# Seven half-width products for a pair of hidden blocks, in the last four batches of a linear attention with a cos-gated MLP

## The chip, the core and the metric

The kernel runs on one core of a Trainium2 chip. Its time is the device time of one execution in microseconds. The engines are TensorE (PE in the rows, its weight loads PEld), VectorE (DVE), ScalarE (ACT), GpSimd (POOL) and SyncE (SP), whose queue issues most of the DMAs; ScalarE's queue issues a few.

## What is computed

The reference, cut to its core (8 batches, 8 heads, 576 rows, head size 64; d_model 512, d_ff 2048):

```python
q_s = exp(q - max(q, -1)); q_s /= sum(q_s, -1) + 1e-9        # over d
k_s = exp(k - max(k, 2));  k_s /= sum(k_s, 2) + 1e-9         # over s
kv = einsum('bhsd,bhse->bhde', k_s, v)
attn = einsum('bhsd,bhde->bhse', q_s, kv)
x = attn.transpose(0, 2, 1, 3).reshape(4608, 512)
h = x @ w_in
out = (h * cos(h)) @ w_out
```

q, k and v are fp32; the two weights come in as 8-byte words, which the kernel turns into fp32 values itself. "The first product" below is x @ w_in, "the second" (g = h cos h) @ w_out.

## The kernel before

**Tiling.** 512 of the 576 rows of each batch are worked as one block; the 64 that are left of each of the eight batches go to DRAM (`x_left`) and come back as a ninth block, batch 8. The hidden dimension is cut into 16 blocks f of 128. A unit is one batch and one f; `order` (L922 to L926) lists all 144. Batches 0 and 1 go through f 0 to 7 and then f 8 to 15 in turn, while the weights arrive; batches 2 to 8 go through all 16. A batch b from 2 on so has units 16 b to 16 b + 15.

**Precision.** Each operand of a product is kept as two halves, high and low, in float32r, and a product is three matmuls: high by high, high by low, low by high. In the first product of a unit (`unit1`, `g1`, L928 to L950) four blocks of 128 rows of w_in are summed, so 12 matmuls of 512 columns go into one PSUM tile `h`. ScalarE then counts turns (L954), VectorE takes the rest (L958), ScalarE the cosine (L964), VectorE multiplies by h (`gate`, L970), ScalarE rounds the high half (L979) and VectorE subtracts for the low half (L985). The second product (`unit2`, L1012 to L1051) has 12 matmuls, three for each of four PSUM tiles `acc`, which are kept through a whole batch and copied out at its end (`out_rows`, L1053). Units with u below F2 = 6 make the second product in one fp32 matmul for each tile (L1021).

**Attention of a batch.** `attend` (L1114) makes k's exponentials (`k_exps`), kv (`kv_rows`, `k_steps`), q's softmax (`q_steps`), the transpose of q by way of DRAM for batches from 2 on (`q_out`, `q_in`, `q_blocks`) and x = q kv (`x_steps`, L739 to L897), four head pairs p for each batch. `x_hi` and `x_lo` (L813, L826) split x into its two halves straight from PSUM. The attention of batch b is woven into the units of batch b - 1. For batch 0 it stands alone, as nothing else can run; its 14 loads follow the list `seq` on SP's queue, or on ScalarE's for those in `actq`.

**PSUM.** There are eight tiles of 2 KB a partition: four `acc`, two `att` (attention) and two `h`. One unit's h is drained while the next unit fills the other one.

**SBUF.** Weights w_in and w_out of every f stay in SBUF, in both halves, from their conversion (`convert`, L378) to the end.

**Order.** Every step is entered in a `Plan` (L56) with its engine, an estimated length, what it reads and writes, and for some a due time (`when(pos)`, T0 + unit x pos, L1111). `order` (L157) lists the steps by a schedule that these lengths give, and the kernel is written out in that order by hand; so each engine's queue, and that of SP, has a fixed sequence. At the end (L1217 to L1221) two units of second product stand after the last first product, and the last two units follow tile by tile.

## Time and profile before

| what | us |
|---|---|
| median of three runs (842.96 to 844.15) | 843.15 |
| the profiled execution | 844.75 |
| its span, from the first instruction to the last | 842.9 |
| TensorE busy in the span | 815.1 |
| VectorE busy | 569.9 |
| ScalarE busy | 504.0 |
| GpSimd busy | 42.5 |

The page gives busy times of each engine, 40 slices of the span, the DMA queues, the chain of work that ended last, and the costliest groups of instructions. A matmul's recorded time is longer than the distance to the next one, since matmuls are pipelined; so TensorE's pace is read from starts. A timeline row merges instructions of one line that follow each other: its second number is the time from the first start to the last end. The mean granted clock of TensorE is 0.998.

### The profile page before, as it was taken

The numbers are of one execution on the slowest core, as the hardware profiler recorded it, in microseconds if no ns is written. First come the engines' busy times: TensorE is split into PE (matmuls) and PEld (weight loads), VectorE is DVE, ScalarE is ACT, GpSimd is POOL, SyncE is SP. The second block draws the span as 40 slices with busy tenths as digits, with TensorE's granted clock in tenths as the row PEclk, the third lists the DMA queues.
The fourth block names the chain that finished last, engine by engine and source line by source line (L and its number), as shares of the span: only waits on it lengthen the run. The fifth ranks groups of instructions, "written<-read, shape, count | busy, mean of one in ns | idle before, by whom it ended". The sixth has DMA issues, their size and how long they took to land.

```text
span 842.9 us, 11862 instructions
## 1 busy us (share of the span) xinstructions
PE 815.1 (97%) x4308; PEld 701.5 (83%) x4308; DVE 569.9 (68%) x920; ACT 504.0 (60%) x823; POOL 42.5 (5%) x161
## 2 busy tenths in 40 slices
PE   1899999999999999999999999999999999999997
PEld 1665788888888888888888888888888888888886
DVE  6979999998598558755876587547763454333443
ACT  3889999866456747564766456745743363334331
POOL 1300200001000000010001000000000000000000
PEclk9999999999999999999999999999999999999999
DMA  8891592246264034502450236023410030001001
GB/s 241 261 270 31 161 327 79 75 114 158 74 165 109 17 81 123 119 17 66 115 142 13 64 73 169 23 49 85 134 32 1 4 101 0 1 1 51 1 0 51
DMA packets 167227, 75.76 MB, mean 90 GB/s; under 512 B 111360, under 2 KB 157952, under 8 KB 167168
## 3 DMA queue, kind: packets, MB, share of 16 engines
q1 hardware_dynamic: 163600, 72.48, 31.8%
q10 hardware_dynamic: 3568, 2.52, 1.0%
q8 instruction: 34, 0.56, 0.3%
q14 instruction: 25, 0.20, 0.1%
HBM read 55.31 MB, written 19.66 MB: 89 GB/s over the span
## 4 chain that ended last, share of the span: by engine, by line
PE 88%; ACT 5%; DMA 3%; DVE 1%; issue 1%; SPq 1%; ACTq 0%; DVEq 0%
PE h L948 41%; PE acc L1028 40%; PE x_False L804 3%; PE kv L622 2%; PE acc L1021 2%; DMA q<-in_q_dram 2%; ACT raw_io L392 1%; DMA raw_i<-in_moe_w_in_dram 1%; DMA v_sb<-in_v_dram 1%; ACT kt L964 0%; ACT ghi L979 0%; ACT kt L954 0%; ACT raw_io L397 0%; ACT o L1077 0%; ACT q L712 0%
## 5 line engine op out<-in xcount | busy, mean ns | idle before, releaser
L948 PE MATMUL h<-x,w_i 128*128 128x512 f32 x1056 | 242.7, 381 | 0.8 <-DVE g L970 0.8
L948 PEld LDWEIGHTS h<-x,w_i 128*128 128x128 f32 x1056 | 198.8, 189 | 30.3 <-DVE g L970 1.2
L1028 PE MATMUL acc<-w_o,ghi 128*128 128x512 f32 x744 | 221.7, 380 | 0.3 <-ACT o L1077 0.3
L958 DVE SCALAR_TENSOR_TENSOR kt<-kt,h 128x512 f32<-128x512 int32 x144 | 99.0, 687 | 104.8 <-ACT kt L954 104.3
L954 ACT ACTIVATE kt<-h 128x512 int32<-128x512 f32 x144 | 86.2, 599 | 132.5 <-PE h L948 128.3
L1028 PEld LDWEIGHTS acc<-w_o,ghi 128*128 128x128 f32 x744 | 139.9, 189 | 20.3 <-ACT o L1077 0.7
L1028 PE MATMUL acc<-w_o,glo 128*128 128x512 f32 x372 | 141.1, 379 | 0.0
L970 DVE TENSOR_TENSOR kt<-kt,h 128x512 f32<-128x512 f32 x138 | 94.7, 686 | 57.7 <-ACT kt L964 56.8
L979 ACT CAST ghi<-kt 128x512 fp32r<-128x512 f32 x136 | 84.3, 620 | 76.3 <-DVE kt L970 38.7
L985 DVE TENSOR_TENSOR glo<-kt,ghi 128x512 fp32r<-128x512 f32 x136 | 93.9, 691 | 51.2 <-ACT ghi L979 50.7
L964 ACT ACTIVATE kt<-kt 128x512 f32<-128x512 f32 x144 | 91.5, 635 | 56.8 <-DVE kt L958 56.4
L948 PE MATMUL h<-x,w_io 128*128 128x512 f32 x480 | 109.6, 379 | 0.0
L1028 PE MATMUL acc<-w_io,ghi 128*128 128x512 f32 x344 | 102.8, 381 | 0.0
L948 PEld LDWEIGHTS h<-x,w_io 128*128 128x128 f32 x480 | 90.1, 189 | 12.4
L1028 PEld LDWEIGHTS acc<-w_o,glo 128*128 128x128 f32 x372 | 70.3, 189 | 10.4 <-DVE glo L985 0.4
L1028 PEld LDWEIGHTS acc<-w_io,ghi 128*128 128x128 f32 x344 | 63.8, 189 | 8.7
L1028 PE MATMUL acc<-w_io,glo 128*128 128x512 f32 x172 | 65.2, 379 | 0.0
L1028 PEld LDWEIGHTS acc<-w_io,glo 128*128 128x128 f32 x172 | 32.5, 189 | 4.6
L804 PE MATMUL x_False<-qt,kvw 128*128 128x288 f32 x176 | 35.5, 323 | 0.5 <-ACT kvw L659 0.5
L964 ACT ACT_TABLE_LOAD x26 | 33.4, 1283 | 0.5
L804 PEld LDWEIGHTS x_False<-qt,kvw 128*128 128x128 f32 x176 | 28.7, 195 | 5.8 <-issue 2.1
L560 POOL PARTITION_ALL_REDUCE m<-m x32 | 26.6, 874 | 118.4 <-DVE m L554 107.7
(114 smaller groups left out, 783.0 us busy)
## 6 DMA issues: line engine op xcount, KB each, us to landing
out_dram<-o SPq DMA_DIRECT2D x32, 256.0 KB, 2.1
q<-in_q_dram SPq DMA_DIRECT2D x31, 256.0 KB, 3.4
k<-in_k_dram SPq DMA_DIRECT2D x14, 512.0 KB, 4.2
qb<-q_rows SPq DMA_DIRECT2D x96, 72.0 KB, 2.4
q_rows<-q SPq DMA_DIRECT2D x24, 256.0 KB, 2.3
raw_i<-in_moe_w_in_dram SPq DMA_DIRECT2D x11, 512.0 KB, 5.3
v<-in_v_dram SPq DMA_DIRECT2D x22, 256.0 KB, 3.5
raw_o<-in_moe_w_out_dram SPq DMA_DIRECT2D x10, 512.0 KB, 5.8
```

The lines of the kernel that those rows point to most:

```text
L560: nc.gpsimd.partition_all_reduce(T["m", b, p0][:, hs].rearrange("p h d -> p (h d)"), T["m1", b, p0][:, hs].rearrange("p h d -> p (h d)"), ...
L622: nc.tensor.matmul(x[h * D : (h + 1) * D, odd : odd + vt.shape[1]], t[:, h, c, :], vt, start=(c == CM), stop=(c == CM - 1),)
L804: nc.tensor.matmul(t[:, 0:HALF], a, c[:, cs] if whole else woven(c[:, cs]), start=(n == 0), stop=(n == len(parts) - 1 and not again))
L948: nc.tensor.matmul(o, a, woven(x), start=(c == 0 and n == 0), stop=(c == KC - 1 and n == 2))
L954: nc.scalar.activation(t, T["h", u], AF.Identity, bias=0.25, scale=1.0 / TWO_PI)
L958: nc.vector.scalar_tensor_tensor(t.bitcast(F32), t, -TWO_PI, T["h", u], op0=ALU.mult, op1=ALU.add)
L964: nc.scalar.activation(t, t, AF.Sin, bias=0.5 * math.pi)
L970: nc.vector.tensor_mul(o, t, T["h", u])
L979: nc.scalar.copy(t, T["kt", u].bitcast(F32))
L985: nc.vector.tensor_sub(t, T["kt", u].bitcast(F32), T["gh", u].bitcast(F32))
L1021: nc.tensor.matmul(T["acc", j], T["g", u][:, js], T["wc", "o", f][:, 0], start=first, stop=last)
L1028: nc.tensor.matmul(T["acc", j], a[:, js], woven(w), start=(first and n == 0), stop=(last and n == 2))
```

## The change

Up to batch 4 the products stay as they are. From batch 5 on (`SB=5`) the units come in pairs, f and f + 1, whose first product is a product of a 512 x 256 block of w_in with the 512 columns of x. Both are cut in two each way, which gives four blocks of w_in and four of x, and the four blocks of the result are made with seven products of blocks instead of eight (Strassen's method, in the form with shared sums). A block of x is 256 rows of d_model by 256 of the 512 columns; a product of blocks is 6 matmuls of 256 columns (two blocks of 128 rows, three matmuls each).

- The weight sums are made once, in eight groups (`combine`), one every six units from unit 32 on, and written with the plain blocks to DRAM (`combined`, 56 operands of 128 x 2 x 256 fp32). From batch 5 on each pair reads its seven operands back into the places where w_in's f 6 to 13 stood; f 0 to 5 give room for the sides of x, f 14 and 15 for g of half of the units.
- The sums of x's blocks (`x_parts`): x goes from PSUM to SBUF as fp32 (`x_f32`), four differences are taken for each of two row blocks, and all are split into halves.
- The products (`products`): T1 and B11 are made into the two halves of one PSUM tile, which was the second `att` tile; ScalarE copies B11's half as the start of both h tiles (`seed`) and T1's half to SBUF (`p5_out`); B21 is added on the one h tile, T2 on the other; VectorE adds the sums into the free halves (`add_12`, `add_22`), and T3, B22 and T4 are added on top.
- Each h tile has a PSUM tag of its own, and the attention of batches 6 and 7 has one `att` tile.
- The second product's four tiles are steps of their own from batch 5 on; one unit's second product instead of two stands after the last first product.
- q of batch 0 is loaded in runs of 1 KB (`QF=1`) into places of later weights and put in order by the exponential; the 14 first loads change places and queues. The planner has another model of DMAs and of TensorE's clock at the start, other due times and lengths, and a table `nudge` that moves 276 single steps of the whole order.

The diff, cut to its core:

```diff
@@ -32,24 +32,32 @@
     FN=11,
     KA=(2, 3),
     QP=((0, 0),),
+    QF=1,
     HA=(2,),
     QD=2,
...
+    t0=9.49,
...
     seq=[
-        ("q", 1), ("k", 1), ("k", 2), ("q", 0), ("k", 0), ("i", 0), ("q", 2),
-        ("q", 3), ("v", 2), ("v", 0), ("v", 3), ("k", 3), ("o", 0), ("v", 1),
+        ("q", 1), ("q", 0), ("k", 2), ("k", 1), ("v", 0), ("k", 0), ("q", 2),
+        ("v", 2), ("i", 0), ("o", 0), ("q", 3), ("k", 3), ("v", 3), ("v", 1),
     ],
-    actq=(('k', 1), ('k', 2), ('k', 3), ('o', 0), ('q', 3), ('v', 1)),
-    wwin=2,
...
+    SB=5,
+    att2={'k': (13.17, -6.89), 'kv': (44.48, 2.71), 'q': (47.77, 7.91), 'qt': (15.78, 23.1), 'x': (17.68, 24.78), 'v': (45.54, 5.38)},
+    lead=1.14,
+    step=(0.0, 0.59, 1.0, 0.98, 1.13, 0.74),
+    late=(0.0, 0.13, -0.04, 1.13),
...
+    def take(*places):
+
+        return [*places, *sorted({("turn", x[0]) for x in places})]
...
-    def bank(tag, name):
+    def bank(tag, name, place=None):
+        if tag == "h":
+            return ps.tile([P, 512], F32, tag=f"h{place[1]}", name=name, bufs=1)
+        tag = "att" if tag == "one" else tag
...
+    def x_parts(b, p, xr):
+
+        j, e = p % 2, side(b, p % 2)
+        es, xf = side(b, 2), T["floats", b, p % 2]
...
+        plan.add("ACT", 0.43 if p < 2 else 0.62, hi, reads=[xf], writes=xr)
+        plan.add("DVE", 0.42 if p < 2 else 0.69, lo, reads=[xf], writes=xr)
+        if p >= 2:
+            x0 = T["xr", b, j]
+            for o, x, y in (
+                ((0, 0), (0, 1), (0, 0)), ((0, 1), (1, 1), (0, 1)), ((1, 1), (1, 1), (0, 0)), ((1, 0), (1, 0), (1, 1)),
+            ):
+                plan.add("DVE", 0.42, lambda o=o, x=x, y=y: minus(o, x, y), writes=[xf])
+            plan.add("ACT", 0.62, lambda: hi_of(0), reads=[xf], writes=x0)
+            plan.add("ACT", 0.62, lambda: hi_of(1), reads=[xf], writes=[es])
+            plan.add("DVE", 0.69, lambda: lo_of(0), reads=[xf] + x0, writes=[e])
+            plan.add("DVE", 0.69, lambda: lo_of(1), reads=[xf, es], writes=[e])
+        T["xr", b, p] = xr
+        return xr + [e, es]
 
...
+    def products(u, xr, due):
+
+        b, f = order[u][:2]
+        h0, h1 = ring("h"), ring("h")
+        T["hplace", u], T["hplace", u + 1] = h0, h1
+        pb, sp = ("att", 1), ring("p5")
+        first = ((b - SB) * NF + f) * 7 // 2
+        n0 = -(-first // 2)
...
+            plan.load(
+                [1.6], load, reads=[(*x, "combined", k) for k in (2 * m, 2 * m + 1) for x in ((), ("low",))], writes=[piece(n)],
+                due=when(u - CFG["lead"]),
+            )
...
+        def product(o, which, dst, start=False):
+            wh, wl = operand(o)
+            for j in range(2):
+                xh, xl = moving(j, which)
+                cs = slice(j * P, (j + 1) * P)
+                for n, (w, x) in enumerate(((wh, xh), (wh, xl), (wl, xh))):
+                    nc.tensor.matmul(
+                        dst(), w[:, cs], x.rearrange("p a i -> p i a"),
+                        start=start and j == 0 and n == 0, stop=j == 1 and n == 2, skip_group_check=True,
+                    )
...
+        def seed(k):
+            T["h", u + k] = bank("h", f"h_{u + k}", (h0, h1)[k])
+            nc.scalar.copy(half(k, 0), pair(0))
+
+        def p5_out():
+            T["p5", u] = sbt([P, TH], F32, "p5", f"p5_{u}")
+            nc.scalar.copy(T["p5", u], pair(1))
+
+        def add_12():
+            nc.vector.tensor_add(half(0, 1), half(1, 0), T["p5", u])
+
+        def add_22():
+            nc.vector.tensor_add(half(1, 1), half(1, 0), T["p5", u])
+
...
+        A, us = CFG["step"], 0.675
+        last = ["last"] if u == len(order) - 2 else []
+        plan.add("PE", us, p5, reads=reads(0), writes=[pb], due=due + A[0])
+        plan.add("PE", us, lambda: product(1, "B11", lambda: pair(0)), reads=reads(1), writes=[pb], due=due + A[0])
+        plan.add("ACT", 0.43, lambda: seed(0), reads=[pb], writes=[h0])
+        plan.add("PE", us, lambda: product(2, "B21", lambda: half(0, 0)), reads=reads(2), writes=[h0], due=due + A[2])
+        plan.add("ACT", 0.43, lambda: seed(1), reads=[pb], writes=[h1])
+        plan.add("PE", us, lambda: product(3, "T2", lambda: half(1, 0)), reads=reads(3), writes=[h1], due=due + A[2])
+        plan.add("ACT", 0.43, p5_out, reads=[pb], writes=[sp])
+        plan.add("DVE", 0.42, add_12, reads=[h1, sp], writes=[h0])
+        plan.add("PE", us, lambda: product(4, "T3", lambda: half(1, 0)), reads=reads(4), writes=[h1], due=due + A[4])
+        plan.add("DVE", 0.42, add_22, reads=[sp], writes=[h1])
+        plan.add("PE", us, lambda: product(5, "B22", lambda: half(0, 1)), reads=reads(5), writes=[h0], due=due + A[4])
+        plan.add("PE", us, lambda: product(6, "T4", lambda: half(1, 0)), reads=reads(6), writes=[h1] + last, due=due + A[5])
...
+    def combine(a, due):
+
...
+        plan.load([0.8] * 2, lambda: keep(0), reads=W[:1], writes=[("combined", o0 + 1), ("combined", o0 + 2)], due=due)
+        plan.load([0.8], lambda: keep(1), reads=W[1:], writes=[("combined", o0 + 6)], due=due)
+        for i in range(2):
+            plan.add("DVE", 0.69, lambda i=i: whole(i), reads=W[i : i + 1], writes=[C], due=due)
+        for s in (s1, s3, s2, s4):
+            plan.add("DVE", 0.42, s, writes=[C], due=due)
+        for i in range(2):
+            s = ring("stage")
+            ops = [("combined", o0 + o) for o in ((3, 5), (4, 0))[i]]
+            plan.add("ACT", 0.62, lambda i=i: hi(i), reads=[C], writes=[s], due=due)
+            plan.add("DVE", 0.69, lambda i=i: lo(i), reads=[s], writes=[C], due=due)
+            plan.load([0.4] * 2, lambda i=i: put(i, T["sumhi", a, i].bitcast(F32), 0), reads=[s], writes=ops, due=due)
+            plan.load([0.4] * 2, lambda i=i: put(i, T["sum", a][:, i], 1), reads=[C], writes=[("low", *x) for x in ops], due=due)
...
-        turn = ["last"] if u >= len(order) - 4 else []
-        if first or last or end:
+        turn = ["last"] if u >= len(order) - (3 if b >= SB else 4) else []
...
+        if 32 <= u < SB * NF and (u - 32) % (2 * (SB - 2)) == 0 and SB <= B:
+            combine((u - 32) // (2 * (SB - 2)), when(u + 2.0))
+        if b >= SB:
+            A = CFG["step"]
+            if f % 2:
+                continue
+            if u - 3 in G:
+                unit2(u - 3, G.pop(u - 3), when(u + A[1]))
+            if b not in X:
+                if b < B:
+                    X[b] = attend(b, (b - 1) * NF, ("one",) * 3 if b > SB else ("att",) * 3)
+                else:
+                    X[b] = sum((left(p, when((B - 1) * NF + 4 + 2 * n)) for n, p in enumerate((0, 2, 1, 3))), [])
+            xs = sorted(set(X[b]), key=str)
+            products(u, xs, when(u))
+            for n in (u, u + 1):
+                G[n] = unit1(n, xs, None)
+            unit2(u - 2, G.pop(u - 2), [when(u + A[3] + x) for x in CFG["late"]])
+            continue
...
     for u in (NU - 4, NU - 3):
-        unit2(u, G[u], when(u + 2.4))
+        if u in G:
+            unit2(u, G[u], when(u + 2.4))
```

## Rows read from the trace of the kernel before

**Rows 1.** The page, part 1: busy us of each engine, share, instructions.

```profile
PE 815.1 (97%) x4308; PEld 701.5 (83%) x4308; DVE 569.9 (68%) x920; ACT 504.0 (60%) x823; POOL 42.5 (5%) x161
```

**Rows 2.** Windows of the span: length, busy us (instructions), clock, DMA share, GB/s.

```profile
0.00:15.00 15.00, 1.30 (x5) 0.93 (x5) 9.97 (x46) 3.89 (x5) 2.29 (x12) 1.00 0.83 218
15.00:30.00 15.00, 8.05 (x63) 5.93 (x63) 12.75 (x27) 10.17 (x25) 3.83 (x7) 1.00 0.94 281
233.00:320.00 87.00, 87.00 (x483) 76.54 (x482) 63.83 (x105) 51.71 (x84) 5.25 (x26) 1.00 0.39 96
496.00:583.00 87.00, 87.00 (x482) 76.53 (x481) 56.67 (x91) 52.13 (x82) 5.25 (x26) 1.00 0.31 76
670.00:755.00 85.00, 85.00 (x396) 74.43 (x395) 36.80 (x53) 35.32 (x58) 0.00 (x0) 1.00 0.08 25
755.00:838.00 83.00, 83.00 (x386) 72.70 (x385) 34.21 (x50) 30.32 (x51) 0.00 (x0) 1.00 0.05 17
```

**Rows 3.** Chain of waits, in order of time: start, us, what, matmuls.

```profile
258.95 2.59 PE h L948 x12
261.54 2.59 PE acc L1028 x12
```

**Rows 4.** Waits: who, for whom, us in total, times, longest us.

```profile
ACT kt L954 <- PE h L948: 128.3, 87, 4.4
...
PE qt L755 <- DVE q L723: 14.2, 2, 13.6
...
PE kv L622 <- DMA v_sb<-in_v_dram: 4.5, 1, 4.5
```

**Rows 5.** Timeline of TensorE, small matmuls: first start, us, what, count.

```profile
54.92 0.60 PE L755 MATMUL qt<-ident,q 128*128 128x128 f32 x4
55.36 0.27 PE L759 MATMUL qt<-ident,q 128*128 128x128 f32 x1
...
561.29 0.90 PE L804 MATMUL x_False<-qt,kvw 128*128 128x288 f32 x6
562.02 1.24 PE L948 MATMUL h<-x,w_io 128*128 128x512 f32 x5
```

**Rows 6.** Groups by form: busy us, mean ns of one, idle before.

```profile
L567 DVE TENSOR_TENSOR k<-k,m 128x1280 f32<-128x1280 f32 x14 | 20.8, 1487 | 0.2 <-POOL m L560 0.2
...
L573 ACT ACTIVATE k<-k 128x1280 f32<-128x1280 f32 x14 | 17.8, 1274 | 0.2
...
L573 ACT ACT_TABLE_LOAD x12 | 15.4, 1283 | 0.2
...
L818 ACT CAST x<-x_False 128x288 fp32r<-128x288 f32 x32 | 12.7, 397 | 4.5 <-PE x_False L804 4.4
L832 DVE TENSOR_TENSOR x<-x_False,x 128x288 fp32r<-128x288 f32 x28 | 12.6, 451 | 1.2 <-ACT x L818 1.2
```

**Rows 7.** Timeline of all engines, last units: start, us, what.

```profile
820.34 5.34 PE L948 MATMUL h<-x_l,w_io 128*128 128x512 f32 x24
...
823.19 0.60 ACT L954 ACTIVATE kt<-h 128x512 int32<-128x512 f32 x1 [2.25 <-PE h L948]
823.82 0.69 DVE L958 SCALAR_TENSOR_TENSOR kt<-kt,h 128x512 f32<-128x512 int32 x1 [2.15 <-ACT kt L954]
824.54 0.63 ACT L964 ACTIVATE kt<-kt 128x512 f32<-128x512 f32 x1 [0.75 <-DVE kt L958]
825.20 0.69 DVE L970 TENSOR_TENSOR kt<-kt,h 128x512 f32<-128x512 f32 x1 [0.70 <-ACT kt L964]
...
825.52 0.59 PE L1028 MATMUL acc<-w_io,ghi 128*128 128x512 f32 x2
...
829.36 0.68 DVE L985 TENSOR_TENSOR g<-kt,g 128x512 fp32r<-128x512 f32 x1
```

**Rows 8.** Timeline of TensorE, the start of the first product.

```profile
36.62 0.59 PE L948 MATMUL h<-x,w_i 128*128 128x512 f32 x1
```

**Rows 9.** Window with the most bytes moved, columns as in rows 2.

```profile
110.00:118.00 8.00, 8.00 (x39) 7.01 (x38) 7.92 (x12) 8.00 (x14) 0.00 (x0) 1.00 1.02 337
```

394 lines of the change are left out of this document (303 added, 91 removed).

## The prediction

> **What bounds the kernel now.** I read the page's first part, then the busy time by stage, then the chain of waits, then who waits for whom. The first shows TensorE busy for 815.1 of 842.9 us and nothing else over 68% [rows 1]. That share is a modelled one, so the stages matter: in each of the four batches shown TensorE is busy for the whole window, at a granted clock of 1.00 (the 2.4 GHz level), while VectorE has 23 to 49 us and ScalarE 35 to 53 us free in each [rows 2]. The chain of waits is there a plain alternation, 2.59 us of the first product (twelve matmuls) and 2.59 us of the second (twelve), with nothing between [rows 3]. So a matmul of 512 columns takes 2.59/12 = 215.8 ns and a unit (one batch, one block of 128 hidden columns) 5.18 us. Who waits confirms it: ScalarE waits 128.3 us for the first product; TensorE's largest waits, 14.2 and 4.5 us, are in the first 20 us, where the attention of batch 0 must come first [rows 4]. What counts is therefore how long TensorE's own stream is, plus the start, plus the tail after its last matmul.
>
> **Part 1: seven products for eight.** From batch 5 on a pair of units made the first product with 24 matmuls of 512 columns, 5.18 us. It now makes seven products of six matmuls, 42 matmuls of 256 columns, each with a weight load of its own. No row shows 256 columns. The nearest above is the 288-column matmul of the attention: six start in 562.02 - 561.29 = 0.73 us, 121.7 ns each [rows 5], each with its own weight load, as every matmul here (4308 of both) [rows 1]. Between 288 and 512 columns the price is (215.8 - 121.7)/224 = 0.42 ns a column, which puts 256 at 108.3 ns. The nearest below is the 128-column transpose: four in 0.44 us, 110 ns [rows 5]. As that is no cheaper than the line gives for 256, something other than columns may hold it, and 110 is the most cautious near value. I take 109 ns, between the two; the ends are 108.3 and 121.7, and a price below the line has no row for it. A pair is then 42 x 0.109 = 4.58 us instead of 5.18, 0.60 less, and 32 pairs (four batches of eight) give **-19.2 us** (ends -20.2 and -2.2). The second product keeps its 24 matmuls. All of this lies on the path, as TensorE has no gap there [rows 2, 3].
>
> A page speaks against this step. The Trainium skill, "TensorE: Matmul & The Clock Gate", section "Back-to-back issue gap", puts a sustained stream of weight load and matmul at about 81 ns for 128 columns and 131 ns for 512. A third of the way along that line (an estimate from the page) 256 columns would cost 98 ns, so 42 of them 4.1 us against 3.1 us for 24 of 512, and the change would lose 31 us. Here 512 columns cost 215.8 ns and 288 cost 121.7 [rows 3, 5], so the trace disagrees and its slope decides; what such a fixed part of each matmul would do here, sized from rows, is the third rival.
>
> **Part 2: what a pair adds beside TensorE.** Three ScalarE copies and two VectorE additions on 128x256. The nearest forms are the 128x288 cast at 397 ns and the 128x288 subtraction at 451 ns [rows 6]: 1.2 and 0.9 us a pair, 9.5 and 7.2 us a batch. The sides of x for each batch add on ScalarE two casts of 128x256 and six of 128x512 (some 4.5 us), on VectorE ten half-size and six full-size subtractions for eight small ones (some 5 us). In the batch with the most other work VectorE is busy 56.7 and ScalarE 52.1 of 87 us [rows 2]; they become about 69 and 66 of some 82, so 84% and 80%. Neither becomes the bound by its sum.
>
> Once, in batches 2 to 4, eight groups of weight sums cost VectorE some 4.4 us and ScalarE 1.2 us each (four full and four half-size operations; two casts). That is 12 us of VectorE a batch where it has 23 free [rows 2], under a TensorE that waits for nothing: 0. If that cover were gone, each late gate would show one to one. Their DMA, 88 issues on SP, writes 14.7 MB.
>
> **Part 3: the chain of a pair.** Before, one unit's PSUM tile was drained while the next was filled. Now a pair owns both h tiles, and the next pair can fill them only when both are drained. Its length, from one unit alone near the end: the twelfth matmul's slot ends at 820.34 + 2.59 = 822.93, the turn count starts at 823.19, and the gate ends at 825.20 + 0.69 = 825.89, so 2.96 us [rows 7]. Then the seed copy with a hop on either side (0.40 + 0.26), T2's product (0.65), an addition with two hops (0.26 + 0.45 + 0.26), T3's product, an addition again and T4's product: 2.96 + 0.66 + 3 x 0.65 + 2 x 0.97 = 7.5 us. The hop out of TensorE is 823.19 - 822.93 = 0.26; that into it has no row of its own and is set equal, an estimate. TensorE's work per pair is 4.58 + 5.18 = 9.76 us, so 2.2 us of slack where the engines have little else.
>
> In batches 5 and 6 the attention of 6 and 7 is woven in, and ScalarE switches tables: 1.283 to exp, 1.27 for the exponential of k, 1.283 back, 3.84 us [rows 6]. The pair is longer there by the attention's own matmuls (87 - 82.9 = 4.1 us or more a batch, 0.5 a pair, against 755 to 838 of [rows 2]), so its slack is 2.7 us and one such group exceeds it by some 1.1. Two groups for k and two for q in two batches are eight: 0 if the order puts each into ScalarE's free part, 9 us if none is. A VectorE operation of 1.49 us (k's subtraction) [rows 6] alone stays within the slack. I take **+3.5 us**, because the rows of before show ScalarE free for 35 us a batch, and keep 0 and 10.
>
> Queued behind a late seed on ScalarE are the casts to hi of the same pair and the next exponential; who waits is TensorE, with the second product of earlier units to fill.
>
> **Part 4: the tail.** Before, the last first product ended at 825.52 and the last lo at 829.36 + 0.68 = 830.04, 4.5 us later, under two units of second product, 5.18 us [rows 7]. Now only one unit's, 2.59 us, stands after the last product, and two units finish together. **+1.5 us** (0 to 2.5).
>
> **Part 5: the start and the single steps.** Batch 0's q is loaded in long runs, its loads change places on SP's and ScalarE's queues (v of pair 0, two DMAs, moves from tenth to fifth of fourteen), and several hundred steps carry a nudge. Of the 27.8 us that TensorE is idle, 20.7 lie before 30 us (13.7 up to 15 us, 7.0 after) [rows 1, 2], and the first product starts only at 36.62 [rows 8]; so what another order can give back lies at the start. The 4.5 us wait for v [rows 4] is what the earlier v and the shorter q can shorten. I take **-2.5 us**, half of that wait and little else, with +2 (the moved loads delay k) and -6 as ends.
>
> **Part 6: the loads of combined weights.** A batch reads back 56 operands of 262 KB, 14.7 MB, 1.84 MB a pair. The busiest stretch moves 337 GB/s at a share of 1.02 [rows 9], so 5.6 us of 9.76, or 57%; the 31% of batch 5's own traffic [rows 2] leaves room: 0. On SP these loads stand in one queue with the attention's stores and reloads of q, which wait for VectorE; the eight places hold operands for 2.3 pairs, some 22 us, so such a wait holds up nothing that is needed soon.
>
> **The sum.** 844.75 us is the profiled execution: span 842.9 and 1.85 around it. -19.2 + 3.5 + 1.5 - 2.5 = -16.7, so 828.05. It lay 1.6 above the median of 843.15, so the forecast of the median is **826.4 us**, with its own range from 819 to 833.
>
> **The rivals.**
> - Attention in the chain: every table switch misses its gap and takes a waiting VectorE operation with it, 1.1 + 1.5 = 2.6 us, eight times, 21 us in place of 3.5; midway, some 13 us, gives 836. For it: VectorE at 84%, no second pair of tiles. Against: half a batch of free ScalarE.
> - The slower end, the loop itself: ScalarE and VectorE run in order, and where hi and lo of both units stand ahead of the seeds and additions, 2 x 0.62 + 2 x 0.69 = 2.6 us enter each pair's chain. 7.5 + 2.6 = 10.1 is still under the old 10.36; it decides from 2.9 us of queueing on. With one more operation of 0.69 and its hop, 11.1, each of 32 pairs is about 0.7 slower than before: 843 + 23 + 1.5 - 2.5 = 865. Against: nothing forces that order, as lo is needed a pair later. The Trainium skill says in "Perfetto Trace Analysis", section "Optimizing Tensor Performance", that independent groups of matmuls should rotate through PSUM banks, so that one is drained while the next is filled; the change gives up part of that, and no run yet shows what that costs here.
> - Small matmuls save nothing: a weight load holds them at the 121.7 ns of the 288-column form, a pair stays at 5.11 us, and -2.2 + 3.5 + 1.5 - 2.5 leaves 843.5. Against: weight loads of transposes follow each other at 110 ns [rows 5].
> - DMA: at batch 5's own efficiency, 76 GB/s for 0.31, a full share moves 245 GB/s; the operands then take 7.5 us of some 10.2 and with 0.31 exceed 1. That batch lengthens by 4% (3.5 us), and late operands add as much: some 833.
>
> **Chances.** Forecast 0.64, attention 0.16, DMA 0.05, no saving 0.04, loop 0.11. Faster by over 0.2% (about what a measurement of this kernel can tell from no change) is 0.85, same 0.04, slower 0.11. The range that leaves out no more than 2 in 10 is the forecast's own with most of the DMA case and half of the attention case: 817 to 836.
>
> **What would show it.** Right: six matmuls of a product start in some 0.655 us; the last batch takes about 78 us instead of 83; TensorE's idle time from batch 5 on is a few microseconds, ended by seeds and additions. Wrong: product matmuls at 120 ns; TensorE idle for over 0.7 us in every pair; a wait of TensorE for combined operands; the first product later than 37 us.

## The result, and the profile after

The changed kernel took **834.7 us** (median of 4 runs, 832.8 to 835.5), the kernel before 843.65 in the runs beside it: a ratio of 0.9884, 95% interval 0.987 to 0.9897, so 9.0 us faster. The forecast was 826.4, or 16.7 us faster, with a range of its own of 819 to 833, and of 817 to 836 with parts of two rivals. Measured a second time beside the last experiment it took 832.97 (832.32 to 833.01) against 844.47: 0.9862 (0.9847 to 0.9877), 11.5 us faster. The first time lies in the wider range alone, the second at the upper end of the narrower one, and the gain is 54 to 69% of the forecast one. Of the 40 runs of the kernel before that stand beside the experiments, 15 have a mean granted clock of 1.000 and a median of 843.3 us, and 23 have one of 0.998 or less and a median of 844.5; beside the second measurement six of seven are of the latter kind, so about 1 of the 11.5 us lies there.

The page of the changed kernel, part 1 (busy us, share, instructions) and the first queue of part 3 (packets, MB, share of 16 engines), against [rows 1]:

```profile
PE 800.4 (96%) x4884; PEld 706.0 (85%) x4884; DVE 635.1 (76%) x1084; ACT 539.2 (65%) x964; POOL 43.3 (5%) x161
...
q1 hardware_dynamic: 193184, 145.92, 59.9%
```

TensorE has 576 matmuls more and is still the bound; the span is 833.5 us, and the profiled execution took 835.5. The same view by windows, columns as in [rows 2]:

```profile
15.00:30.00 15.00, 9.22 (x81) 7.13 (x82) 11.91 (x25) 12.25 (x30) 1.63 (x3) 1.00 0.93 285
...
30.00:60.00 30.00, 25.85 (x193) 19.07 (x193) 27.10 (x47) 28.96 (x59) 4.31 (x8) 1.00 0.98 294
60.00:102.00 42.00, 41.24 (x187) 27.57 (x187) 39.56 (x64) 36.81 (x69) 3.42 (x5) 1.00 0.41 125
102.00:125.00 23.00, 21.04 (x96) 17.46 (x95) 18.32 (x28) 20.46 (x31) 1.99 (x2) 1.00 0.98 316
...
490.00:573.00 83.00, 81.32 (x600) 75.64 (x599) 65.54 (x113) 55.39 (x109) 5.09 (x6) 1.00 0.78 230
573.00:655.00 82.00, 82.00 (x622) 76.84 (x621) 60.89 (x106) 50.46 (x105) 1.78 (x20) 1.00 0.88 249
655.00:740.00 85.00, 85.00 (x570) 79.46 (x570) 50.36 (x91) 46.77 (x94) 0.00 (x0) 1.00 0.67 208
740.00:829.00 89.00, 89.00 (x578) 82.52 (x577) 45.39 (x74) 40.04 (x82) 0.00 (x0) 1.00 0.49 147
```

The first Strassen product starts at 486.8 us. From 490 us to 829 TensorE is busy but for 1.7 us, at the same granted clock of 1.00 as before; what it loses beyond that lies before 180 us. In 30 to 60 us it is idle for 4 us while ScalarE is busy for 28.96 of 30, VectorE for 27.10 and the DMA engines for a share of 0.98.

Who TensorE waited for (columns as in [rows 4]):

```profile
PE qt L925 <- DVE q L811: 12.3, 1, 12.3
PE kv L695 <- ACT k L646: 7.6, 3, 5.0
PE h L1144 <- DVE kt L1166: 2.7, 4, 1.6
PE h L1144 <- ACT x L1008: 1.9, 1, 1.9
PE h L1259 <- DVE h L1285: 1.7, 1, 1.7
```

Only the last row belongs to a Strassen product (line 1259). One product and what follows it, in the timeline of TensorE, against [rows 5]:

```profile
705.47 0.83 PE L1259 MATMUL h<-x,w_io 128*128 128x256 f32 x6
706.14 0.60 PE L1387 MATMUL acc<-w_o,ghi 128*128 128x512 f32 x2
```

Six matmuls of 256 columns take 706.14 - 705.47 = 0.67 us, 112 ns each, where the forecast had 0.655.

To see where time went I added up, from the starts of all matmuls of a trace, what their spacing exceeds the steady one of their form by (215.8 ns for 512 columns, 112 for 256, 123 for 288, 109 for transposes, 429 for the undivided fp32 products of the first units and, on average, 34 for the small matmuls of kv), together with the time before the first matmul. This is TensorE's lost time up to a point of the span, in us; the lines below "again" are the experiments told further down. What a lower granted clock costs is counted as lost too:

```
                        60    102    125    180    490    end
before                33.9   36.5   36.4   37.6   37.4   37.4
changed               34.2   37.3   40.1   41.7   41.6   43.2
changed, again (e12)  34.4   37.3   39.4   40.9   40.8   40.3
e1  late stores       34.0   36.1   38.6   40.1   40.0   39.8
e2  no Strassen       33.2   34.9   35.3   37.4   37.9   37.9
e3  no moved steps    32.2   36.5   39.0   40.6   42.3   43.3
e5  head              35.1   37.6   39.8   41.4   41.2   41.3
e6  queue             34.5   36.8   38.4   40.0   39.9   41.1
e7  e1 + e5 + e6      34.7   36.9   38.4   39.9   40.4   40.6
e8  q in pieces       34.8   37.8   40.5   42.0   41.9   42.6
e9  woven             33.7   35.8   38.6   40.1   41.3   65.2
e10 longer chain      34.3   37.0   42.8   44.0   43.9   64.8
e11 e1 + e6           33.8   35.9   37.5   39.0   38.8   39.0
```

The matmuls themselves save 768 x 0.2158 - 1344 x 0.112 = 165.7 - 150.5 = 15.2 us. The changed kernel's first profile gives 4.2 of that back by 490 us and 1.6 after it: -15.2 + 4.2 + 1.6 = -9.4, which is the difference of the spans, 833.5 - 842.9. The second profile gives back 3.4, and loses 0.5 less than before after 490 us: -12.3, spans 830.5 and 842.9 (-12.4).

The row of the kernel before holds a stretch at a granted clock of 0.50 (the 1.2 GHz level), from 31.0 to 34.4 us, that neither profile of the changed kernel has. By the two medians in the first paragraph it is worth some 1.2 us, an estimate, so a run of the kernel before without it would have lost about 36.4 us by 180.

### The profile page after: what moved, and what is told of

It is laid out like the page before. It is cut to its first block, busy times and chain, and to the rows that moved or that the text cites. A ratio compares the mean times of both kernels' runs of the same rounds, so it can differ in the third digit from the quotient of the medians.

```text
span 833.5 us, 13731 instructions
## 1 busy us (share of the span) xinstructions
PE 800.4 (96%) x4884; PEld 706.0 (85%) x4884; DVE 635.1 (76%) x1084; ACT 539.2 (65%) x964; POOL 43.3 (5%) x161
## 4 chain that ended last, share of the span: by engine, by line
PE 80%; ACT 6%; DVE 5%; DMA 5%; issue 2%; SPq 1%; ACTq 0%; DVEq 0%
PE acc L1387 39%; PE h L1144 19%; PE h L1259 13%; PE pb L1259 5%; PE x_False L974 2%; PE kv L695 2%; DMA v<-in_v_dram 1%; DMA k<-in_k_dram 1%; ACT raw_io L449 1%; DMA q<-in_q_dram 1%; ACT raw_io L454 1%; DMA combined<-w_i 1%; PE acc L1380 1%; DMA raw_o<-in_moe_w_out_dram 1%; DVE k L640 1%
## 5 line engine op out<-in xcount | busy, mean ns | idle before, releaser
L1387 PE MATMUL acc<-w_o,ghi 128*128 128x512 f32 x552 | 164.8, 380 | 0.1
L1144 PE MATMUL h<-x,w_i 128*128 128x512 f32 x660 | 154.0, 383 | 4.3 <-DVE kt L1166 2.4
L1387 PEld LDWEIGHTS acc<-w_o,ghi 128*128 128x128 f32 x552 | 100.5, 189 | 13.0 <-ACT o L1437 0.8
L1387 PE MATMUL acc<-w_o,glo 128*128 128x512 f32 x276 | 104.6, 379 | 0.0
L1387 PE MATMUL acc<-w_o,w_io 128*128 128x512 f32 x288 | 70.7, 379 | 0.0
L1144 PE MATMUL h<-x,w_io 128*128 128x512 f32 x300 | 68.9, 379 | 0.2 <-DVE kt L1166 0.2
L1144 PEld LDWEIGHTS h<-x,w_io 128*128 128x128 f32 x300 | 56.2, 189 | 8.3 <-DVE kt L1166 0.6
L1387 PEld LDWEIGHTS acc<-w_o,w_io 128*128 128x128 f32 x288 | 51.2, 190 | 5.3
L1259 PE MATMUL h<-x,w_i 128*128 128x256 f32 x320 | 47.7, 275 | 1.7 <-DVE h L1285 1.7
L1259 PE MATMUL h<-w_i,w_i 128*128 128x256 f32 x280 | 44.5, 276 | 0.0
```

Source lines behind the costliest of these rows:

```text
L1144: nc.tensor.matmul(o, a, woven(x), start=(c == 0 and n == 0), stop=(c == KC - 1 and n == 2))
L1259: nc.tensor.matmul(dst(), w[:, cs], x.rearrange("p a i -> p i a"), start=start and j == 0 and n == 0, stop=j == 1 and n == 2, skip_group_c ...
L1387: nc.tensor.matmul(T["acc", j], a[:, js], woven(w), start=(first and n == 0), stop=(last and n == 2))
```

## The experiments

The theory at the outset: the combine's stores of plain weight blocks, issued from 31.7 us on, crowd the first batches' loads; the rival: the new order and start lose the time themselves.

**e1, late stores.** The order is left alone but for the two steps with the stores of plain blocks of each group:

```diff
+    for k0, k1, put0, put1 in late:
+        steps = [i for i in steps if i not in (k0, k1)]
+        at = steps.index(put0)
+        steps[at:at] = [k0, k1]
     with tc.manual_schedule():
         for i in steps:
```

> The changed kernel with one thing moved: the 24 stores of 256 KB that put the plain blocks of the weights into DRAM are issued on SP's queue just before their group's first store of a sum, instead of from 31.7 us on between the loads of the first batches. Nothing else changes. Theory A (those 6.3 MB compete with the first batches' loads while the DMA engines are busy over 0.9 of the time, so operands land late and TensorE loses about 5 us by 180 us): the gain is 2 to 5 us, 830 to 833 us; the DMA share of 30 to 60 us falls from .99/.97 to at most .93, and TensorE's idle above its usual in 102 to 145 us falls from 2.3 us to under 1. Rival B (the early loss comes from the new order and the new start, not from the stores): within 1 us of the changed kernel, 834 to 836 us, with the same late units.

Measured: 832.56 us (831.53 to 834.93), ratio 0.9868 (0.9851 to 0.9885). The stores now start at 208 us, and the DMA share of 30 to 60 us falls from 0.98 to 0.86. TensorE loses 2.1 us instead of 3.1 between 60 and 102 us, and 2.5 instead of 2.8 between 102 and 125; for 102 to 145 theory A wanted under 1 in place of 2.3. The 2.1 us of the medians looked like theory A at its low end; e12 takes that back.

**e2, without Strassen and moved steps; e3, without moved steps.** They bracket Strassen's method by itself and the moved steps by themselves; the first of the two changes below is e2's alone, the second (its long line cut here) is in both.

```diff
-    SB=5,
+    SB=9,
...
-    nudge={7: -2.2, 12: -2.2, 26: -3.4, 29: -10.3, 48: 4.1, 49: -13.7, 55: 1.6, 66: -4.3, ...
+    nudge={},
```

> The changed kernel with Strassen's method off for every batch (no combined weights, no sums of x; the first product is made of 48 matmuls of 512 columns in all batches) and without the moved single steps; the new planner, the new start and the one PSUM tile for each bank stay. To be compared with the kernel of the next run, which is the same with Strassen's method on. My forecast puts Strassen's own part (matmul -19.2, chain +3.5, tail +1.5) at -14.2 us; with 112 ns for a matmul of 256 columns it is -15.4 + 1.9 = -13.5. Theory A (the combine's stores cost the early loss of 5 us): this kernel takes 841 to 844 us, and Strassen's method with its stores is worth only -8 to -10. Rival B (the new order and start cost it): this kernel takes 847 to 850 us, slower than the kernel before, and Strassen's method is worth its -13.5.

> The changed kernel without the moved single steps (the table of them is empty); everything else stays. Theory A (the moved steps take small waits away, at most one of 0.3 to 1 us in some of the places where the trace of the changed kernel has no wait): 836 to 840 us. Rival (they are near nothing, as my forecast of 0 to -1 us for them had it): 834 to 836 us. A third: they have a cost, since they were laid out for other times: 832 to 834 us.

Measured: e2 844.43 us (843.48 to 845.59), ratio 1.0006 (0.9997 to 1.0014), so the new planner, start and PSUM tiles are worth nothing by themselves. All of e2's twelve runs have a granted clock of 0.999 or 1.000; against the 843.3 of the kernel before at 1.000 they cost some 1.1 us. Neither theory A (841 to 844, with 8 to 10 us for Strassen's method) nor rival B (847 to 850) has both numbers right. e3 took 839.48, ratio 0.994 (0.992 to 0.996); its six runs lie in two groups, 835.4 to 835.5 (two) and 839.4 to 840.3 (four), and its profile is of the first group. So Strassen's method without the moved steps gains 844.43 - 839.48 = 5.0 us (9.0 in e3's shorter runs), and the moved steps gain the other 4.8 (against 834.7) to 6.5 (against 832.97). Against e3's shorter runs they gain only 0.7 to 2.5, and the profile, being of such a run, cannot show more. By the median theory A for the moved steps held at its upper end. The profiles of e2 and e3 also show when Strassen's order costs: e2 has lost 35.3 us by 125 us, e3 39.0, though no Strassen product runs before 490.

**e4, what sets 112 ns.** Five of the seven small products of each pair are cut down in three batches (batch 6: 224 moving columns; batch 8: 192; batch 7: 64 weight columns, 256 moving):

```diff
+                    if which not in ("T1", "B11") and b in (6, 8):
+                        k = {6: 112, 8: 96}[b]
+                        o, m = o[:, 0 : 2 * k], m[:, 0:k]
+                    if which not in ("T1", "B11") and b == 7:
+                        o, cs = o[0:64], slice(j * P, j * P + 64)
```

> The changed kernel, with the five of the seven small products that stand apart made smaller in three batches, which leaves part of the output unfilled: in batch 6 with 224 moving columns instead of 256, in batch 8 with 192, in batch 7 with 64 weight columns instead of 128 and all 256 moving ones. Batch 5 is left whole. It asks what sets the 112 ns of a matmul of 256 columns with weights of its own. Theory A (the weight load of 128 columns does, the moving columns fit under it): 110 to 112 ns in batches 6 and 8 as well, and under 112, near 109, in batch 7. Rival B (the moving columns do, at 0.42 ns each plus a few): 98 ns in batch 6, 84 in batch 8, 112 in batch 7. Rival C (something fixed for each instruction): 112 in all.

Measured, in one run of 832.37 us, from TensorE's timeline, batch 7 and then batch 8:

```profile
693.71 0.82 PE L1265 MATMUL h<-x,w_i 128*64 128x256 f32 x6
694.36 0.82 PE L1265 MATMUL h<-w_i,w_i 128*64 128x256 f32 x6
...
745.35 0.25 PE L1265 MATMUL h<-x,w_io 128*128 128x192 f32 x1
745.44 0.28 PE L1265 MATMUL h<-w_i,w_io 128*128 128x192 f32 x1
745.55 0.39 PE L1265 MATMUL h<-x,w_io 128*128 128x192 f32 x2
...
747.34 0.80 PE L1265 MATMUL h<-w_i,w_io 128*128 128x192 f32 x6
747.98 0.62 PE L1393 MATMUL acc<-w_io,ghi 128*128 128x512 f32 x2
```

With 64 weight columns a product starts 0.65 us after the one before. With 192 moving columns the first matmul behind one of 512 is followed after 0.09 us, the next after 0.11. Over the whole trace, from start to start: 112 ns at 192, 224 and 256 moving columns alike (212, 212 and 562 matmuls that follow one of their kind), 109 ns with 64 weight columns and 256 moving ones (216); directly behind a matmul of 512 columns 83, 96 and 109 ns. So the moving columns alone would take 83/192 = 0.43 ns each, and the load of 128 weight columns holds a stream of small matmuls at 112. Theory A is shown. What the first small matmul of a stream saves is not kept: a matmul of 512 columns behind one of 192 takes 245 ns and behind one of 224 takes 232, so 29 and 16 ns more than 216, and 112 - 83 = 29, 112 - 96 = 16.

**e5, the head.** VectorE's steps for the second pair of query heads go behind what was queued behind them, and so does their exponential on ScalarE:

```diff
+    for mv_, at_, k_ in [([55, 48, 56, 57, 58], 86, 0), ([144, 41], 55, 0), ([145], 86, 0), ([49, 43, 59, 146], 88, 0)]:
+        steps = [i for i in steps if i not in mv_]
+        k_ += steps.index(at_)
+        steps[k_:k_] = mv_
```

> The changed kernel with single steps of batch 0 in another order: on VectorE the maximum and the subtraction of the second pair of query heads (lines 780 and 784, which wait 4.49 us for their load at 13.5 to 18 us) come behind the steps of the keys and the inverse of kv that were queued behind them, and on ScalarE the exponential of that pair comes behind the two exponentials of keys and the copy of kv. Nothing else changes. Theory A (the earlier start is lost in this queue): kv of pair 1 is at 17 to 18 us instead of 23.25, the first product at 28 to 31 us instead of 33.32, and the time falls by 1.5 to 3 us, to 832 to 833. Rival B (ScalarE, busy over .94 from 30 us on, or the loads set this stretch, so an earlier step is waited away later): TensorE's work at 60 us stands within 0.5 us of the changed kernel's and the time is 834 to 835.5.

Measured: 833.65 us (833.51 to 834.97), ratio 0.9882 (0.9867 to 0.9897). Two of TensorE's waits:

```profile
PE kv L695 <- ACT k L646: 3.3, 3, 1.9
PE kv L695 <- ACT kvw L732: 2.6, 1, 2.6
```

The window of 30 to 60 us, which is as full on ScalarE as in the changed kernel:

```profile
30.00:60.00 30.00, 26.74 (x190) 20.03 (x189) 26.94 (x49) 28.93 (x59) 4.60 (x9) 0.94 0.97 287
```

The wait of kv for k's exponential falls from 7.6 to 3.3 us, 2.6 of it come back as a wait for another ScalarE step, kv of pair 1 starts at 21.07 (not 17 to 18) and the first product at 34.33, where the changed kernel's two profiles have 33.32 and 34.46. At 60 us TensorE has lost 35.1 us, 0.7 to 0.9 more than unchanged. Rival B: the wait that the trace named could be removed, and the stage did not get shorter. The 0.94 in the row is a granted clock of 0.50 from 47.2 to 50.6 us, in which 26 matmuls of the first product take 7.5 us instead of 5.8. That is not what the result rests on: they start at 45.80, behind a wait for ScalarE, and in the changed kernel at 44.81 and 45.03, so the stage is late before the clock falls; and of the 1.7 us, 1.0 to 1.3 stand in the changed kernel as a wait behind these matmuls, which e5 does not have.

**e6, the queue.** Three loads of weights go into SP's gap at 91 us, and batch 7's key maxima behind the Strassen additions (the three lines below this one are as in e5):

```diff
+    for mv_, at_, k_ in [([528, 579, 567], 552, 1), ([2728, 2729, 2730], 2112, 1)]:
```

> The changed kernel with two moves that lie 430 us apart, so that the trace tells them apart. First, three loads of weights (512 KB each) go on SP's queue into the gap at 91 to 96 us instead of behind the value and query loads of batch 2 at 97 to 107 us. Second, VectorE's three key maxima of batch 7 (line 618 at 539.7 us, which waits 2.90 us for its load) come behind the two additions of the Strassen products that were queued behind them. Theory A (queue order alone makes these stalls): TensorE's stalls at 106 and 110 us (0.46 and 1.78) fall under 0.5 in sum, the one at 540 us (1.84) is gone, and the time falls by 3 to 4 us, to 831 to 832. Rival B (the DMA engines, busy .98 from 102 to 125 us and .88 later, are short in themselves): the stall at 110 us comes back as another, later load's, the chain waits for the moved key steps later on, and the time falls by under 1 us.

What it aims at, in ScalarE's timeline of the changed kernel:

```profile
106.99 0.63 ACT L1177 CAST ghi<-kt 128x512 fp32r<-128x512 f32 x1
110.01 0.73 ACT L449 ACTIVATE raw_o<-raw_o 128x512 f32<-128x512 f32 x1 [2.39 <-DMA raw_o<-in_moe_w_out_dram]
110.64 0.61 ACT L1160 ACTIVATE kt<-kt 128x512 f32<-128x512 f32 x1
```

The load that it waited for, in the timeline of SP's queue:

```profile
103.95 0.43 SPq L426 DMA_DIRECT2D raw_o<-in_moe_w_out_dram  x1
```

The weights issued at 103.95 land at 110, ScalarE waits 2.39 us for them with the cosine of the next gate behind, and TensorE waits 1.6 us for that gate. After the move, the window:

```profile
102.00:125.00 23.00, 22.29 (x102) 18.56 (x101) 19.23 (x28) 22.18 (x32) 1.45 (x2) 1.00 0.84 271
```

and what is left of TensorE's wait in it:

```profile
PE h L1144 <- DVE kt L1166: 0.3, 1, 0.3
```

The wait is nearly gone and TensorE loses 1.6 us there instead of 2.1 to 2.8. The stall at 540 us is gone too, but 1.2 us of smaller ones (at 527, 532 and 546) stand in its place. The time is 833.29 (832.92 to 833.83), ratio 0.9875 (0.986 to 0.989): 1.4 us under the first measurement, 0.3 over the second. What was local in theory A held; the gain of 3 to 4 us did not come.

**e7, all three together.**

> The late stores of the first experiment with the moves of the two before this one together. If the three causes are apart, their gains add: 2.1 us of the late stores plus 1.5 to 3 of the head plus 2 to 3 of the queue, less the stall at 540 us that the first experiment had lost already: 828 to 830 us. If one limit stands behind all three (the DMA engines or ScalarE in the first 180 us), it is 831 to 833.

Measured: 834.19 us (833.13 to 835.01), ratio 0.9886 (0.9869 to 0.9902). Nothing adds: 39.9 us lost by 180 us, as in e6 alone (40.0) and e1 alone (40.1). That is the rival, and past its upper end.

**e8, queries in pieces.** Three conditions, order kept:

```diff
-                if flat:
+                if False:
...
-            if flat:
+            if False:
...
-                if not flat:
+                if True:
```

> The changed kernel with the queries of batch 0 loaded as the kernel before did, in pieces of 256 bytes straight to their place, instead of in rows that ScalarE's exponential puts in place; the order of all steps is kept. Theory A (the loads in rows bring the start forward): first matmul 13.2 to 13.8 us instead of 12.27, and the time rises by 0.5 to 1.4 us. Rival B (the second pair's load ends last for VectorE either way, and the start is lost there): the first matmul is later all the same, but the work done at 60 us and the time stay within 0.5 us.

Measured: 834.55 us (833.83 to 835.52), ratio 0.989 (0.9875 to 0.9905). The first matmul moves from 12.27 to 13.41 us. At 60 us 34.8 us are lost instead of 34.2 to 34.4. A start that is 1.1 us later costs 0.4 to 0.6 us at 60 us, and in the time at most the spread of one kernel between two measurements: nearer to rival B.

**e9, woven.** The six matmuls of a small product are issued in turn with those of a neighbouring step of the second product:

```diff
+        while small or big:
+            for x in small[:r]:
+                nc.tensor.matmul(*x[0], **x[1])
+            small = small[r:]
+            for x in big[:1]:
+                nc.tensor.matmul(*x[0], **x[1])
+            big = big[1:]
```

> The kernel of the first experiment (late stores), with 126 of the 224 small products woven with the matmuls of 512 columns that stand next to them in TensorE's order: two of 256 columns and one of 512 in turn, or one and one. What is computed and all other engines' order stay; 561 instead of 121 matmuls of 256 columns now follow one of 512. Theory A (back to back, a matmul of 256 columns waits for its own weight load, 112 ns; behind a matmul of 512 the load is done in its 216 ns): these 440 matmuls fall from 112 to 109 ns, those of 512 stay at 216, TensorE's sum falls by 1.3 us, and the time, by 0 to 1.5 us, to 831 to 832.5. Rival B (112 ns is what any matmul of 256 columns with its own weights takes): no change of the sum; 832 to 833.5, as the chain of a pair is lengthened by at most 0.65 us for each product.

Measured: 856.4 us (855.6 to 858.2), ratio 1.0148 (1.013 to 1.0165), slower than both kernels. From start to start 559 matmuls of 256 columns behind one of 512 do stand at a median of 109 ns, but 567 of 512 behind one of 256 stand at 218 instead of 216: two of the three nanoseconds come back. The 24 us beside e1 lie in 62 gaps of over 0.1 us between matmuls. Of these, 12.9 us are waits of the products (lines 1380 and 1393) for the seed copies of ScalarE (line 1278) and 2.8 for the additions (line 1285); the list of waits names nothing for the rest. The largest:

```profile
PE h L1393 <- ACT h L1278: 12.4, 19, 1.3
```

and one of these in TensorE's timeline:

```profile
692.12 0.81 PE L1380 MATMUL acc<-w_o,w_io 128*128 128x512 f32 x3
693.47 0.38 PE L1393 MATMUL h<-w_i,w_i 128*128 128x256 f32 x1 [0.54 <-ACT h L1278]
```

A product that is spread over 1.3 us instead of 0.67 ends later, and the chain of the pair runs through several of them. This asked for a test of the chain itself.

**e10, a longer chain.**

```diff
-            nc.scalar.activation(t, T["h", u], AF.Identity, bias=0.25, scale=1.0 / TWO_PI)
+            for _ in range({7: 2, 8: 4}.get(b, 1)):
+                nc.scalar.activation(t, T["h", u], AF.Identity, bias=0.25, scale=1.0 / TWO_PI)
```

> The changed kernel with a longer chain from a Strassen pair's products to its gates: ScalarE's first step on each unit's h (line 1150, about 0.55 us of its engine) is done twice in batch 7 and four times in batch 8, with the same result. A pair's chain becomes longer by up to 1.1 us in batch 7 and 3.3 us in batch 8, eight pairs in each. My forecast gave the chain 2.2 us of slack for a pair and took 3.5 us for what it would cost all the same. Theory A (slack as worked out): batch 7 loses under 0.5 us of TensorE's time, batch 8 loses about 1.1 us for each pair, 6 to 9 us in all: 841 to 844 us. Rival B (no slack; the chain is at its limit already): batch 7 loses 6 to 9 us as well, batch 8 some 20 or more: over 855 us. Rival C (more slack than worked out, since the order of TensorE puts more second products behind a pair than counted): both batches lose under 1 us: 834 to 836 us.

Measured, one run: 856.98 us. A pair of batch 8 in the timeline of all engines:

```profile
791.18 2.50 ACT L1151 ACTIVATE kt<-h 128x512 int32<-128x512 f32 x4
793.58 0.62 ACT L1161 ACTIVATE kt<-kt 128x512 f32<-128x512 f32 x1
...
795.04 0.36 ACT L1279 COPY h<-pb 128x256 f32<-128x256 f32 x1
...
795.45 0.94 PE L1260 MATMUL h<-x,w_i 128*128 128x256 f32 x6 [2.35 <-ACT h L1279]
```

The windows of batch 7 and of batch 8:

```profile
655.00:740.00 85.00, 85.00 (x566) 78.95 (x565) 51.34 (x92) 55.89 (x111) 0.00 (x0) 1.00 0.68 209
740.00:855.00 115.00, 96.71 (x589) 85.83 (x587) 46.17 (x76) 68.32 (x132) 0.00 (x0) 0.97 0.40 123
```

A step takes 2.50/4 = 0.62 us, so a pair's chain is longer by up to 2 x 0.62 = 1.2 us in batch 7 and by up to 3.7 in batch 8. Batch 7 loses 0.1 us in all. Batch 8 loses 19.9, or 2.5 a pair, 10.3 of it as waits of a product for the seed copy behind the longer step. Some 3.5 of the 19.9 is another thing: from 769.0 to 772.4 and from 796.3 to 799.7 us, each time soon after a wait of TensorE (1.99 and 2.35 us), the granted clock is 0.50, and the matmuls there take 8.0 us instead of 4.55. Without it the loss is some 2 us a pair. So the slack is 1.2 to 1.7 us a pair, an estimate: theory A in batch 7, theory A's mechanism with little over half its slack in batch 8. Rival B had the total (over 855) and batch 8 (some 20), but batch 7, which it had at 6 to 9, rules out that there is no slack.

The clock fell once more in this run, far ahead of what was changed:

```profile
102.00:125.00 23.00, 19.42 (x82) 16.06 (x81) 15.82 (x25) 17.82 (x28) 1.73 (x2) 0.93 0.96 303
...
113.43 4.54 PE L1144 MATMUL h<-x,w_i 128*128 128x512 f32 x12 [3.27 <-DVE kt L1167]
```

Twelve matmuls need 4.38 us from 113.43 to the next start at 117.81 instead of 2.59, so 1.8 of the 5.8 us that e10 loses between 102 and 125 us are the clock's.

**e11, late stores and queue; e12, the changed kernel again.**

> The late stores of the first experiment with both moves of the sixth (three loads of weights earlier on SP's queue; VectorE's key maxima of batch 7 behind the Strassen additions), without the moves at the head. To be set against the changed kernel, which runs again beside it. Theory A (two causes, stores and queue order, each with its own stalls): the gains of some 1.6 us that each had by 180 us add in part, 830.5 to 832 us, 2.5 us or more under the changed kernel. Rival B (one limit behind them: ScalarE and VectorE, busy over .9 from 30 to 180 us, so that TensorE waits for a gate whichever load comes sooner): TensorE's idle at 180 us is 27 to 28 us as in each of the two alone, and the time is 832 to 833.5.

> The changed kernel itself, again, beside the run before it: what one and the same order varies by. Expected: 833.5 to 835.5 us, with TensorE's idle by 102 us within 0.7 us of the first profile's 25.0 and the stretch of 102 to 125 us, where the same order lost 2.2 to 5.8 us in the profiles of kernels that differ only elsewhere, the place that varies most. If it falls to 832 or 833, the gains of 1 to 2 us that single experiments showed are no more than chance.

Measured: e11 832.73 us (831.24 to 832.99), ratio 0.9862 (0.9846 to 0.9879); e12 832.97, ratio 0.9862 (0.9847 to 0.9877). By the trace e11 has lost 39.0 us at 180 us, 1.9 less than e12, which suggests that stores and queue order together cost TensorE something; but e11's profile is of its shortest run (831.24, the others 832.7 to 833.0), and in time, as rival B has it, the two kernels cannot be told apart. The differences of 1 to 2 us that e1, e5 and e6 seemed to show are about as large as the 1.7 us that the changed kernel's own two medians lie apart. None of the versions beats the changed kernel by more than that. The stall at 540 us of the first profile is absent from e12, where TensorE is busy for all of the window:

```profile
490.00:573.00 83.00, 83.00 (x616) 77.54 (x616) 67.80 (x116) 55.02 (x109) 4.43 (x6) 1.00 0.79 234
```

## Why the prediction was right, and where its size was off

**Bound and mechanism: right.** TensorE's own stream is the bound, seven products for eight shorten it on the path, and by the trace the gain lies in the Strassen batches alone. That the time lies in the stated range is in part luck: 834.7 is above the forecast's own 833, in the part of the range that was given to the rivals of attention and DMA, and neither of the two came true as described.

**Part 1, -19.2: mis-sized, -15.2.** The step that failed is the choice of 109 ns "between the two". The line through 288 and 512 columns was right for the columns (e4: 83, 96 and 109 ns behind a long matmul). But the prediction had itself seen that the 128-column transposes at 110 ns [rows 5] were no cheaper than the line gives for 256, "so something other than columns may hold it", and then did not take that something as a floor. It is one: 112 ns for each matmul of the small products with 128 weight columns of its own, whether it moves 192, 224 or 256 columns (e4). The transposes themselves, by their starts, stand 109 ns apart. The third rival named the mechanism and had the price too high (121.7). The Trainium skill, "TensorE: Matmul & The Clock Gate", section "LDWEIGHTS (loading the stationary operand)", gives the load as the number of weight columns divided by 1.2, in ns; by that formula, as an estimate, it is 107 for 128 and 53 for 64. The runs agree with it as a floor, within 5 ns: 112 ns with 128 weight columns, and no floor above the 109 of the moving columns with 64. The estimate of 98 ns that the prediction drew from the section "Back-to-back issue gap" of the same page of the Trainium skill is contradicted by 112.

**Part 2, 0: right in the Strassen batches, wrong in its place before them.** VectorE and ScalarE are busy for 65.5 and 55.4 of 83 us in the fullest batch, where the forecast had 69 and 66 of 82, so ScalarE's part was put some 11 us too high. The weight sums were taken to lie in batches 2 to 4. Their stores of plain blocks begin at 31.7 us, in a stage with a DMA share of 0.98; taking them away from there gave TensorE about 1 us between 60 and 102 us (e1), and no difference in time that could be measured.

**Part 3, +3.5 (0 to 10): 0 to 2, and the slack mis-sized.** After 490 us the profiles with unchanged products lose between -0.5 and 1.6 us net. The one large stall, in the first profile, is not the rival of the table switches: VectorE waited 2.9 us for keys, with the addition that TensorE needed queued behind. In the changed kernel's chain that ended last these keys, and the end, are:

```profile
530.90 8.81 DMA k<-in_k_dram
...
820.14 9.08 PE acc L1387 x42
```

The load took 8.81 us in a stretch with a DMA share of 0.78, where the page's median for this load is 4.4; in e12 it did not hold VectorE. That the slack was enough is luck: 2.2 us worked out, 1.2 to 1.7 measured (e10). The second rival, the loop, decides therefore sooner than from 2.9 us of queueing. e9 and e10 show what it does once the chain is full (products late behind their seeds, 24 and 20 us), though there the chain was lengthened by the products and by a longer step, not by casts queued ahead of the seeds as the rival had it.

**Part 4, +1.5: 0.** After the last small product TensorE runs 42 matmuls without a gap, as the second row above shows; both last gates fit under them. From the last matmul's start to the span's end it is 4.6 us before and after.

**Part 5, -2.5 (-6 to +2): wrong, +3.4 to +4.2.** This is the largest miss. In the two profiles the first matmul came 1.35 and 1.2 us and the first product 3.3 and 2.2 us earlier, as hoped, but nothing of it was left at 60 us (33.9 before, 34.2 and 34.4 after; without its stretch at a clock of 0.50 the kernel before would have some 32.7, an estimate). The step that failed is that an idle TensorE at the start was read as time that an earlier start gives back. The 4.5 us wait for v went, and a longer one for k's exponential, 7.6 us in the rows above, came in its place; in the kernel before it was

```profile
PE kv L622 <- ACT k L573: 1.6, 1, 1.6
```

The clock also rose later. In the kernel before TensorE works from 19.44 us on with small gaps and is granted 1.00 from 24.1 us; in the changed kernel it waits 4.96 us until 23.25 and is granted 1.00 from 27.3 us, and from 29.4 in the second profile. Four matmuls of the attention on either side of that step in the changed kernel:

```profile
24.54 2.29 PE L974 MATMUL x_False<-qt,kvw 128*128 128x288 f32 x4
...
29.58 1.14 PE L974 MATMUL x_False<-qt,kvw 128*128 128x288 f32 x4
```

Besides, ScalarE was nearly full from 30 to 60 us before as well, in a window that none of the forecast's rows shows:

```profile
30.00:60.00 30.00, 28.78 (x215) 21.42 (x215) 24.32 (x44) 28.25 (x62) 4.22 (x7) 0.94 0.87 262
```

The front of the stage moved, and by that reading the other engines set its end. e5 and e8 agree with it from both sides; how the loss divides between the later clock and the full engines is not shown. But by 60 us only 0.3 to 0.5 of the 3.3 to 4.1 us are there that the changed kernel has lost by 180 us beyond the kernel before. The rest is a term that the forecast does not have: most of it falls between 102 and 125 us, where weights were queued behind values and queries. e2, with the start and the planner alone, has lost 37.4 by then, no more than the kernel before with its low clock and some 1 us more than without it, so the 3.5 to 4.3 us beyond e2 belong to the order laid out with Strassen's steps in it. Of these e11 removes 1.9 in the trace of its shortest run. The moved steps, taken at near nothing, are worth 4.8 to 6.5 us of median; without them the whole change would have gained 4 us.

**Part 6, 0: right.** The DMA share of the Strassen batches is 0.49 to 0.88, and 0.78 in batch 5, for which 0.31 + 0.57 was worked out, and TensorE waited for no combined operand.

**The sum.** -15.2 for -19.2, 0 to 2 for the +5 of chain and tail, and +3.4 to +4.2 for -2.5. Two cautious terms repaid a third to a half of what the two hopeful ones lost.

**Open.** Why three fixes that each remove their wait do not add (e7): its four runs have granted clocks of 0.995 to 0.998, where those of e1 and e11 have 0.999 and 1.000, and its profile was granted 0.50 from 28.4 to 31.9 us, so part of it may be the clock, which no run takes apart; what loses the remaining 1.4 us by 180 us in e11; why the clock falls in some executions of one order and not in others; and why e3 has two groups of times 4 us apart, as its profile is of one of the shorter runs (three of the four longer ones have a clock of 0.996 to 0.998, the fourth 1.000).

## What to carry to other kernels

Before halving a matmul's moving columns, ask what its weight load costs back to back: the gain stops at that floor, and a small matmul anywhere in the trace (here a transpose, at 109 ns) already comes close to showing it. Time that an engine idles in a stage where two others are nearly full need not be given back by an earlier start or by removing the wait that the trace names. Look at the granted clock of each short stretch before a loss there is put down to a wait. And before a fix of 1 to 2 us is believed, the unchanged kernel has to run beside it again.

## What the runs showed of the hardware

- A stream of the small products with a load of 128 weight columns each stays at 112 ns from start to start at 256, 224 and 192 moving columns; with 64 weight columns 256 moving ones take 109. Only the first behind a matmul of 512 columns is faster (109, 96, 83 ns), and the matmul of 512 behind the last of them gives nearly all of that back: 218, 232 and 245 ns instead of 216. The 128-column transposes, with 128 weight columns, stand at 109.
- One and the same order of this window lost between 2.1 and 5.8 us in 102 to 125 us (the changed kernel twice, 2.8 and 2.1; e5 2.2; e8 2.7; e10 5.8, whose change lies 500 us later and of which 1.8 is the clock's), in a window where the DMA engines were busy for a share of 0.98 to 1.02 in the changed kernel's two profiles. The kernel before, at 0.98 in the same window, lost nothing there.
- Soon after a wait of TensorE the granted clock fell to 0.50 in some places (e10 at 113.6, 769.0 and 796.3 us, after waits of 3.27, 1.99 and 2.35; e5 at 47.2 and e6 at 46.2, after one of 1.9; the kernel before at 31.0, after one of 1.65) and not in others (the changed kernel after 44.8 us, behind the same wait of 1.91; e10 after 783.6, behind 2.35). In every window of the changed kernel from 30 us on that is shown above it was 1.00.
- At the start of the span the rows print 1.00 where TensorE ran at half of that: transposes stand 213 ns apart before 24.1 us in the kernel before and before 27.3 us in the changed kernel, and 109 ns after.
